# Reordering the opening of a fused Fourier-mixing and gated-cosine kernel on Trainium2: x by two queues first, z's first column group ahead, weight folds inside the steps

## The chip, the cores and the metric

The kernel runs on one core of one Trainium2 chip. The metric is the device time of one execution in microseconds. Before the change three runs gave 1979.25, 1980.98 and 1982.95 us, a median of 1980.98 us.

## The reference

Two parts are computed one after the other, all in float32. x has the shape (8, 3008, 256).

```
X = fft(fft(x, axis=1), axis=2);  y = real(X)            # 8 x 3008 x 256
h = y.reshape(24064, 256) @ w_in                         # w_in 256 x 2048
g = h * cos(h)
out = g @ w_out                                          # w_out 2048 x 256
```

## The kernel before, in words

**How the work is split.** A sequence of 3008 is 47 times 64, so the transform along the sequence is done in two halves. The *first half* multiplies by a table L of 47-point cosines and sines: x is laid out with the 47 index s2 on the partitions (rows 0 to 46 hold 32 of the 64 positions s1, the next 47 rows hold the mirrored other ones), four tiles `xp` of eight positions each per batch, and each tile is two chunks. For a chunk, `fold` (L212) adds and subtracts the mirrored columns of the feature axis into `xf`, `first_half` (L233) makes the products with L into a PSUM bank `pz` and ScalarE copies it to `zs` (L262). z must change its layout, and this goes through DRAM: `store_z` (L268) writes `zs` to `zd`, `load_z` (L280) reads it back as `z2`. The *second half* (`second_half`, L292) multiplies `z2` with the table BJ, one of six column groups g at a time, into `pq`. The transform along the features is folded into the weights: `fold_weights` (L351) multiplies w_in with a cosine and sine table CS into WC and WS, 512 columns (a *quarter*) at a time, and `take_wn` (L364) sums up the row of WS that belongs to the Nyquist feature into `wn` and then lets GpSimd clear that row (L376).

**The steps.** A *step* is one batch b, one column group g and one pair fp of the 16 slices of 128 of the 2048 hidden columns: 8 batches times 6 groups times 8 pairs are 384 steps (L709 to L715). Group 0 has 225 columns, the others 256. In the loop at L724 a step goes through four ages: `seed` (L420, ScalarE writes the Nyquist term and 0.25 into the PSUM bank H), `mm1` (TensorE, L439, cosine part and sine part), `act_e`, `dve_h`, `act_round`, `dve_frac`, `act_sin`, `dve_g`, `dve_s` (ScalarE and VectorE make g times cos for four mirrored outputs), and, three steps later, `mm2` (TensorE, L531: seven products per step, a fast form with the combined weights VX and w2). `combine_w2` (L408) makes VX from w_out on VectorE, a quarter per call.

**What sets the order.** The schedule is manual: the order of the calls is the order on each engine's queue, and every engine works its queue strictly in that order. All loads, and all stores but two at the very end, are issued by SyncE (SP). The work of the next batch's transform is put into the steps by `transform` (L330), and the work of the first batch that isn't needed at once by the table `opening` (L699): its key is a step, and its calls come at the end of that step (L771).

**The opening.** Before the loop stands a list of calls (L642 to L698). SP's order in it is: L, the first x tile, CS, the first quarter of w_in, the second x tile; then the first column group of z (columns 0 to 4 of 24) of chunks 0 and 1; then w_in's second quarter and x tiles 2 and 3; z of chunks 2 and 3; w_in's third quarter, the first part of BJ; then the other columns of z of chunks 0 and 1, and so on; at last the first column group is read back, and after it the rest of z, w_out, the last quarter of w_in and the rest of BJ. TensorE folds the quarters 0, 1 and 2 in this list (L649, L661, L685) and quarter 3 in step 0 (L700, L732). `keep_busy` (L394) gives TensorE products without a use. For group 0 of batch 0 the Nyquist row is spread over the partitions by a product with ones and a ScalarE copy (L320, L323), ahead of the first seed; for all other groups by a store of one row and a load of it to all partitions (L326, L327). The loads of one x tile are, for rows r0 to r1 of 0 to 32 and 32 to 47:

```python
nc.sync.dma_start(
    out=xv[r0:r1], in_=x_r[b, r0:r1, i0 : i0 + XP, :], max_dma_last_dim=2048
)
q0, q1 = N2 + r0, N2 + r1
...
nc.sync.dma_start(
    out=xv[q0:q1], in_=x_r[b, r0:r1, 64 - i0 : 64 - i0 - XP : -1, :]
)
```

so the direct rows lie on partitions 0 to 46 and the mirrored ones on 47 to 93, and the rows of L are in the same order. In the direct part a row of a tile is one run of 8 KB in DRAM, in the mirrored part it is eight runs of 1 KB.

Of the kernel before, what the change touches and what calls it, by code (L numbers as in the profile page):

```python
# [11 lines left out]
FP = mybir.dt.float32  # L12
# [19 lines left out]
def _consts():  # L32
# [19 lines left out]
    L = np.concatenate([LE, LO, LE0, LO0], axis=1)  # L52
    L = np.concatenate([L, np.zeros((128 - 2 * N2, 256))], axis=0)

# [53 lines left out]
def kernel(  # L108
# [30 lines left out]
    def load_x(b, p):  # L139
# [5 lines left out]
        for r0, r1 in ((0, 32), (32, 47)):  # L145
# [3 lines left out]
            q0, q1 = N2 + r0, N2 + r1  # L149
            if p == 0:  # L150
                nc.sync.dma_start(out=xv[q0:q1, 0:1], in_=x_r[b, r0:r1, 32:33, :])
                nc.sync.dma_start(
                    out=xv[q0:q1, 1:XP], in_=x_r[b, r0:r1, 63 : 64 - XP : -1, :]
                )
            else:
                nc.sync.dma_start(
                    out=xv[q0:q1], in_=x_r[b, r0:r1, 64 - i0 : 64 - i0 - XP : -1, :]
                )
# [14 lines left out]
    def load_w(q):  # L173
        for i in range(2):
            nc.sync.dma_start(
# [15 lines left out]

    nc.sync.dma_start(out=L, in_=L_dr.ap())
    load_x(0, 0)
    load_cs()
    load_w(0)
    load_x(0, 1)
# [15 lines left out]
    def fold(b, c, e):  # L212
# [13 lines left out]
        if e:  # L226
            nc.scalar.copy(
# [64 lines left out]
    def second_half(b, g):  # L292
# [25 lines left out]
        if b == 0 and g == 0:  # L318
            pn = psum("pn", "M")
            nc.tensor.matmul(  # L320
                pn[:, 0:T], lhsT=ones, rhs=pq[0:1, T : 2 * T], start=True, stop=True
            )
            nc.scalar.copy(out=nb[:, 0:T], in_=pn[:, 0:T])  # L323
            return
# [3 lines left out]


# [34 lines left out]
    def take_wn(n):  # L364
# [11 lines left out]
        nc.gpsimd.memset(row, 0.0)  # L376

    def fold_quarter(n):
        fold_weights(1, n)
# [40 lines left out]
    def seed(s):  # L420
# [3 lines left out]
        for u in range(2):  # L424
# [7 lines left out]
            )  # L432

# [208 lines left out]
    keep_busy(2, "H", 512)  # L642
    keep_busy(2, "H", 512)
    chunk(0)
    chunk(1)
    first_half(0, 0)
    chunk(2)
    first_half(0, 1)
    fold_weights(1, 0, "H")  # L649
    fold_weights(0, 0, "H")  # L650
    take_wn(0)
    store_z(0, 0, 0, 4)
    store_z(0, 1, 0, 4)
    load_w(1)
    load_x(0, 2)
    load_x(0, 3)
    chunk(3)
    first_half(0, 2)
    chunk(4)
    first_half(0, 3)  # L660
    fold_quarter(1)  # L661
    store_z(0, 2, 0, 4)
    store_z(0, 3, 0, 4)
    x1 = spool.tile([128, XP * ND], FP, tag="xp", bufs=4, name="wr")
    wr.append([x1[:, 1024 * i : 1024 * i + 1024] for i in range(2)])
    load_w(2)
    load_bj(0, 512)
    store_z(0, 0, 4)
    store_z(0, 1, 4)
    chunk(5)  # L670
    first_half(0, 4)
    chunk(6)
    first_half(0, 5)
    store_z(0, 4, 0, 4)
    store_z(0, 5, 0, 4)
    store_z(0, 2, 4)
    store_z(0, 3, 4)
    chunk(7)
    first_half(0, 6)
    first_half(0, 7)  # L680
    store_z(0, 6, 0, 4)
    store_z(0, 7, 0, 4)
    for half in range(2):
        load_z(0, half, 0, 4)
    fold_quarter(2)  # L685
    keep_busy(2, "M", 256)
    load_w2(0, 2)
    load_w(3)
    load_w2(2, 4)
    for c in range(4, 8):  # L690
        store_z(0, c, 4)
    load_bj(512, 1024)
    for half in range(2):
        load_z(0, half, 4)
    load_w2(4, 6)
    load_w2(6, 8)
    load_bj(1024, NJ * 128)
    second_half(0, 0)  # L698
    opening = {  # L699
        0: ((fold_weights, 0, 3), (take_wn, 3), (combine_w2, 0, 2)),  # L700
        1: ((combine_w2, 2, 4),),
        5: ((combine_w2, 4, 6), (second_half, 0, 1)),
        6: ((combine_w2, 6, 8),),
        10: ((second_half, 0, 2), (load_ident,)),
        14: ((second_half, 0, 3),),
        18: ((second_half, 0, 4),),
        22: ((second_half, 0, 5),),
    }
# [96 lines left out]
```

## Time and profile before

| what | value |
|---|---|
| median of 3 runs | 1980.98 us (1979.25 to 1982.95) |
| profiled execution | span 1979.1 us, 28626 instructions; no other time of it is given |
| TensorE (PE) busy | 1951.8 us, 99% of the span |
| VectorE (DVE) busy | 1855.3 us, 94% |
| ScalarE (ACT) busy | 1483.3 us, 75% |
| GpSimd (POOL) busy | 460.8 us, 23% |
| mean granted clock of TensorE | 0.997 of full speed |
| DMA queue of SP | 86.68 MB, 21.3% of 16 engines |
| first product of step 0 (L439) | starts at 44.39 us |
| first product of step 3 (L439) | starts at 58.66 us |
| first product of step 8, the first of group 1 (L439) | starts at 82.43 us |

How to read the profile: a line of the *timeline* has the start, the duration, the engine, the line of the kernel, the operation, the tile written, an arrow and the tiles read, and how many such instructions in a row are put together; brackets give the idle time before it and what ended it. SPq and ACTq are the queues that issue DMAs, and a duration there is that of the issuing alone. *Stretches* give, for a part of the span, its length, then for TensorE's products (PE), TensorE's weight loads (PEld), VectorE, ScalarE and GpSimd the busy time with the number of instructions, then the granted clock of TensorE, the share of the time in which the 16 DMA engines had a transfer (it can pass 1 where transfers overlap on an engine), and GB/s. The *chain* is followed back from the last instruction to whatever released each piece; its rows are the start, the duration and what it was. float32 products run in several passes, so one call of the program shows as more than one row. All times are from the start of the span.

### The profile page before, as it was taken

Reading aid. Unit: us, or ns where it says so; the run is one execution under the profiler, and the core shown is the slowest. Engines: PE = TensorE matmul, PEld = TensorE weight load, DVE = VectorE, ACT = ScalarE, POOL = GpSimd, SP = SyncE. Lnnn points to the kernel's source line nnn. Section 1 sums busy time; section 2 is a strip of 40 time slices with the busy share of each in tenths; the row PEclk is TensorE's granted clock in tenths of the full one; section 3 lists DMA queues with packets and bytes.
Section 4 is the critical chain, followed back from the end, with each engine's and each line's share of the span. In section 5 each row is a group of like instructions: output and inputs, shape, how many; then the busy total and the mean of one; then the engine's idle time right before and its main releaser. Section 6 shows DMA issues by size and latency. Waiting matters only on the chain.

```text
span 1979.1 us, 28626 instructions
## 1 busy us (share of the span) xinstructions
PE 1951.8 (99%) x9350; PEld 1703.2 (86%) x9350; DVE 1855.3 (94%) x3208; ACT 1483.3 (75%) x2696; POOL 460.8 (23%) x420
## 2 busy tenths in 40 slices
PE   7999999999999999999999999999999999999998
PEld 4888899888998889888898888988889888898887
DVE  2999989999899998999999999899999999899998
ACT  2777777777777777777877778777777777778775
POOL 0132212331133211323122232123311223112111
PEclk9999999999999999999999999999999999999999
DMA  7512122131112311122121311223012220200000
GB/s 181 108 43 57 31 49 41 34 62 39 43 31 41 58 35 43 36 45 54 31 43 40 64 30 35 44 55 55 19 40 49 50 51 20 47 21 10 18 16 22
DMA packets 181194, 88.63 MB, mean 45 GB/s; under 512 B 103303, under 2 KB 173622, under 8 KB 180918
## 3 DMA queue, kind: packets, MB, share of 16 engines
q1 hardware_dynamic: 180886, 86.68, 21.3%
q8 instruction: 75, 1.23, 0.3%
q14 instruction: 73, 0.60, 0.1%
q10 hardware_dynamic: 160, 0.13, 0.0%
HBM read 49.50 MB, written 37.27 MB: 44 GB/s over the span
## 4 chain that ended last, share of the span: by engine, by line
PE 90%; DVE 5%; DMA 2%; issue 1%; ACT 1%; SPq 1%; DVEq 0%; ACTq 0%
PE M L531 53%; PE H L439 31%; PE pz L246 3%; PE pb L299 2%; DVE r L484 1%; DMA xp<-in_x_dram 1%; DVE S L502 1%; DVE S L504 1%; DVE S L495 1%; DVE h L455 1%; DVE r L474 0%; DMA out_dram<-ob 0%; SPq L633 0%; DVE ob L623 0%; ACT r L470 0%
## 5 line engine op out<-in xcount | busy, mean ns | idle before, releaser
L480 ACT ACTIVATE r<-r 128x1024 f32<-128x1024 f32 (+1 forms) x384 | 398.6, 1038 | 306.0 <-DVE r L474 305.2
L531 PE MATMUL M<-S,VX 128*128 128x256 f32 (+1 forms) x2304 | 612.3, 375 | 0.0
L531 PEld LDWEIGHTS M<-S,VX 128*128 128x128 f32 x2304 | 437.8, 190 | 49.9
L439 PE MATMUL H<-pq,WS 128*128 128x256 f32 (+1 forms) x1536 | 390.0, 376 | 10.2 <-ACT ew L450 9.8
L439 PE MATMUL H<-pq,WC 128*128 128x256 f32 (+1 forms) x1536 | 394.8, 380 | 1.8 <-ACT H L426 1.8
L531 PE MATMUL M<-r,w 128*128 128x256 f32 (+1 forms) x1536 | 388.5, 375 | 0.0
L426 ACT ACTIVATE H<-nb,wn 128x256 f32<-128x256 f32 (+1 forms) x768 | 363.8, 474 | 17.4 <-DVE r L484 4.8
L455 DVE TENSOR_TENSOR h<-ew,H 128x512 f32<-128x512 f32 (+1 forms) x384 | 257.2, 670 | 95.2 <-PE H L439 87.3
L439 PEld LDWEIGHTS H<-pq,WS 128*128 128x128 f32 x1536 | 289.5, 190 | 52.5 <-ACT ew L450 16.3
L531 PEld LDWEIGHTS M<-r,w 128*128 128x128 f32 x1536 | 301.2, 197 | 27.1
L474 DVE SCALAR_TENSOR_TENSOR r<-r,h 128x512 f32<-128x512 f32 (+1 forms) x384 | 310.1, 807 | 0.0
L439 PEld LDWEIGHTS H<-pq,WC 128*128 128x128 f32 x1536 | 283.6, 190 | 30.3 <-ACT H L426 2.5
L220 POOL TENSOR_TENSOR xf<-xp 94x508 f32<-94x508 f32 x112 | 165.2, 1495 | 565.9 <-PE pz L253 550.1
L495 DVE TENSOR_TENSOR S<-r 128x512 f32<-128x512 f32 (+1 forms) x384 | 290.9, 758 | 0.1
L484 DVE SCALAR_TENSOR_TENSOR r<-h,r 128x512 f32<-128x512 f32 (+1 forms) x384 | 273.8, 713 | 0.0
L470 ACT ACTIVATE r<-H 128x512 f32<-128x512 f32 (+1 forms) x384 | 222.8, 580 | 56.5 <-DVE h L455 53.4
L450 ACT ACTIVATE ew<-H 128x512 f32<-128x512 f32 (+1 forms) x384 | 225.3, 587 | 48.5 <-PE H L439 44.2
L474 DVE SCALAR_TENSOR_TENSOR r<-r,H 128x512 f32<-128x512 f32 (+1 forms) x384 | 255.6, 666 | 0.0
L484 DVE SCALAR_TENSOR_TENSOR r<-H,r 128x512 f32<-128x512 f32 (+1 forms) x384 | 254.5, 663 | 0.3 <-ACT r L480 0.3
L470 ACT ACTIVATE r<-h 128x512 f32<-128x512 f32 (+1 forms) x384 | 236.2, 615 | 0.0
L531 PE MATMUL M<-r,VX 128*128 128x256 f32 (+1 forms) x768 | 225.2, 375 | 0.0
L531 PE MATMUL M<-S,w 128*128 128x256 f32 (+1 forms) x768 | 225.2, 375 | 0.0
(67 smaller groups left out, 1497.6 us busy)
## 6 DMA issues: line engine op xcount, KB each, us to landing
out_dram<-ob SPq DMA_DIRECT2D x728, 32.0 KB
xp<-in_x_dram SPq DMA_DIRECT2D x56, 256.0 KB
zd<-zs SPq DMA_DIRECT2D x112, 96.0 KB
z<-zd SPq DMA_DIRECT2D x28, 384.0 KB
xp<-in_x_dram SPq DMA_DIRECT2D x56, 120.0 KB
nb<-nd SPq DMA_DIRECT2D x40, 128.0 KB
wr<-in_moe_w_in_dram SPq DMA_DIRECT2D x8, 256.0 KB
w<-in_moe_w_out_dram SPq DMA_DIRECT2D x4, 512.0 KB
```

Of the source, the lines that this page charges most:

```text
L220: (nc.gpsimd if b else nc.vector).tensor_tensor(out=fv[:, e, :, 1:128], in0=xv[:, :, 1:128], in1=xv[:, :, 255:128:-1], op=ALU.subtract if ...
L246: nc.tensor.matmul(pz[rows, a:512], lhsT=w, rhs=fv[:, e, a:512], start=True, stop=True)
L426: nc.scalar.activation(out=s.H[:, u * T : u * T + T], in_=s.nb[:, 0:T], func=AF.Copy, bias=0.25, scale=wn[:, f : f + 1],)
L439: nc.tensor.matmul(s.H[:, u * T : u * T + T], lhsT=W[:, 128 * f : 128 * f + 128], rhs=s.pq[:, e * T : e * T + T], start=False, stop=True, ...
L450: nc.scalar.mul(out=s.ew[:, 0 : 2 * s.T], in_=s.H[:, 0 : 2 * s.T], mul=2.0)
L455: nc.vector.tensor_tensor(out=s.h[:, 0 : 2 * T].rearrange("p (u t) -> p u t", u=2)[:, :, ::-1], in0=s.ew[:, 0 : 2 * T].rearrange("p (u t) ...
L470: nc.scalar.activation(out=r, in_=h, func=AF.Copy, bias=BIG, scale=1.0)
L474: nc.vector.scalar_tensor_tensor(out=r, in0=r, scalar=-BIG, in1=h, op0=ALU.add, op1=ALU.subtract)
L480: nc.scalar.activation(out=r, in_=r, func=AF.Sin, bias=0.0, scale=SIN_SCALE)
L484: nc.vector.scalar_tensor_tensor(out=r, in0=h, scalar=-0.25, in1=r, op0=ALU.add, op1=ALU.mult)
L495: nc.vector.tensor_tensor(out=sv[:, 0:2], in0=gv[:, 2:3].to_broadcast([128, 2, T]), in1=gv[:, 0:4:3], op=ALU.subtract,)
L531: nc.tensor.matmul(acc[key][m // 2][:, 256 * (m % 2) : 256 * (m % 2) + T], lhsT=w, rhs=a, start=first, stop=s.fp == 7, skip_group_check=True,)
```

## The change

Seven things change, all but one before or in the first steps.

1. The x loads of batch 0 are the first DMAs of the program, all four tiles, and the mirrored rows are issued by ScalarE's queue instead of SP's (`back`). L comes after the first tile, then CS, the first quarter of w_in and the first part of BJ. For the other batches SP still issues all.
2. The mirrored rows lie elsewhere: those of rows 0 to 31 on partitions 62 to 93, those of rows 32 to 46 on partitions 47 to 61. The rows of the table L are put in the same order. This holds for all batches.
3. For batch 0 the small copy of two columns into `xf` (L227) is GpSimd's and not ScalarE's.
4. The list of calls is a loop over the eight chunks: fold of the next chunk, first half of this one, store of its first column group. After chunk 1 ScalarE's queue issues the second quarter of w_in. After the loop SP reads the first column group back, then come w_out's first part, w_in's quarters 2 and 3, w_out's second part, the rest of z, and the rest of w_out and BJ.
5. Quarter 0 of the weights is folded after the last chunk; quarters 1, 2 and 3 are folded in steps 0, 1 and 2 (`fold_weights(1, t + 1)` in the middle, `fold_rest` at the end of the step).
6. The first step is not seeded by ScalarE: VectorE fills its bank with 0.25 (`fill_first`), and two products of the one Nyquist row of WS with the Nyquist row of `pq` add the term (`seed_first`); the row of WS is cleared after that (`clear_row`). The spreading of the Nyquist row for the later steps of group 0 moves into step 0 (`spread_norm`).
7. `keep_busy` has one product per call instead of two at the start and none later; in `opening` the second half of group 1 moves from step 5 to step 6, and `combine_w2` of the second quarter of w_out stays in step 1.

```diff
--- before.py
+++ after.py
@@ -50,6 +50,7 @@
     LE0 = stack(np.cos(th), z, z, np.cos(thh))
     LO0 = stack(np.sin(th), z, z, np.sin(thh))
     L = np.concatenate([LE, LO, LE0, LO0], axis=1)
+    L = L[np.r_[0:N2, N2 + 32 : 2 * N2, N2 : N2 + 32]]
     L = np.concatenate([L, np.zeros((128 - 2 * N2, 256))], axis=0)
 
     k2 = np.arange(64)
@@ -142,18 +143,18 @@
         xt = xs[b, p]
         xv = xt.rearrange("r (i d) -> r i d", d=ND)
         i0 = XP * p
-        for r0, r1 in ((0, 32), (32, 47)):
+        back = nc.sync if b else nc.scalar
+        for r0, r1, q0, q1 in ((0, 32, 62, 94), (32, 47, 47, 62)):
             nc.sync.dma_start(
                 out=xv[r0:r1], in_=x_r[b, r0:r1, i0 : i0 + XP, :], max_dma_last_dim=2048
             )
-            q0, q1 = N2 + r0, N2 + r1
             if p == 0:
-                nc.sync.dma_start(out=xv[q0:q1, 0:1], in_=x_r[b, r0:r1, 32:33, :])
-                nc.sync.dma_start(
+                back.dma_start(
                     out=xv[q0:q1, 1:XP], in_=x_r[b, r0:r1, 63 : 64 - XP : -1, :]
                 )
+                back.dma_start(out=xv[q0:q1, 0:1], in_=x_r[b, r0:r1, 32:33, :])
             else:
-                nc.sync.dma_start(
+                back.dma_start(
                     out=xv[q0:q1], in_=x_r[b, r0:r1, 64 - i0 : 64 - i0 - XP : -1, :]
                 )
 
@@ -170,9 +171,9 @@
         for i in range(2):
             nc.sync.dma_start(out=CS[i], in_=CS_dr.ap()[i * 128 : (i + 1) * 128, :])
 
-    def load_w(q):
+    def load_w(q, queue=nc.sync):
         for i in range(2):
-            nc.sync.dma_start(
+            queue.dma_start(
                 out=wr[q // 2][i][:, 512 * (q % 2) : 512 * (q % 2) + 512],
                 in_=moe_w_in[i * 128 : (i + 1) * 128, 512 * q : 512 * q + 512],
             )
@@ -189,11 +190,13 @@
             in_=moe_w_out.rearrange("(q p) c -> p q c", p=128)[:, 2 * f0 : 2 * f1],
         )
 
+    load_x(0, 0)
     nc.sync.dma_start(out=L, in_=L_dr.ap())
-    load_x(0, 0)
+    for p in range(1, 4):
+        load_x(0, p)
     load_cs()
     load_w(0)
-    load_x(0, 1)
+    load_bj(0, 512)
     WC = cpool.tile([128, NDFF], FP, tag="WC", name="WC")
     WS = cpool.tile([128, NDFF], FP, tag="WS", name="WS")
     wn = cpool.tile([128, 16], FP, tag="wn", name="wn")
@@ -224,7 +227,7 @@
             op=ALU.subtract if e else ALU.add,
         )
         if e:
-            nc.scalar.copy(
+            (nc.scalar.copy if b else nc.gpsimd.tensor_copy)(
                 out=fv[:, :, :, 0].rearrange("r e i -> r i e"), in_=xv[:, :, 0:129:128]
             )
 
@@ -316,16 +319,18 @@
         nb = spool.tile([128, 256], FP, tag="nb", bufs=8, name="nb")
         ready[b, g] = (pq, nb)
         if b == 0 and g == 0:
-            pn = psum("pn", "M")
-            nc.tensor.matmul(
-                pn[:, 0:T], lhsT=ones, rhs=pq[0:1, T : 2 * T], start=True, stop=True
-            )
-            nc.scalar.copy(out=nb[:, 0:T], in_=pn[:, 0:T])
             return
         nd = dpool.tile([1, 256], FP, tag="nd", bufs=4, name="nd")
         nc.sync.dma_start(out=nd[:, 0:T], in_=pq[0:1, T : 2 * T])
         nc.sync.dma_start(out=nb[:, 0:T], in_=nd[0:1, 0:T].to_broadcast([128, T]))
 
+
+    def spread_norm():
+        T = _width(0)
+        pq, nb = ready[0, 0]
+        pn = psum("pn", "M")
+        nc.tensor.matmul(pn[:, 0:T], lhsT=ones, rhs=pq[0:1, T : 2 * T], start=True, stop=True)
+        nc.scalar.copy(out=nb[:, 0:T], in_=pn[:, 0:T])
 
     def transform(b):
         todo = {}
@@ -373,10 +378,13 @@
                 stop=True,
             )
         nc.scalar.copy(out=wn[:, 4 * n : 4 * n + 4], in_=pw[:, 0:4])
-        nc.gpsimd.memset(row, 0.0)
-
-    def fold_quarter(n):
-        fold_weights(1, n)
+        if n:
+            clear_row(n)
+
+    def clear_row(n):
+        nc.gpsimd.memset(WS[0:1, 512 * n : 512 * n + 512], 0.0)
+
+    def fold_rest(n):
         fold_weights(0, n)
         take_wn(n)
 
@@ -430,6 +438,24 @@
                 bias=0.25,
                 scale=wn[:, f : f + 1],
             )
+
+    def fill_first(s):
+        s.H = psum("H", "H")
+        nc.vector.memset(s.H[:, 0 : 2 * s.T], 0.25)
+
+    def seed_first(s):
+        T = s.T
+        s.pq, s.nb = ready[s.b, s.grp]
+        for u in range(2):
+            nc.tensor.matmul(
+                s.H[:, u * T : u * T + T],
+                lhsT=WS[0:1, 128 * u : 128 * u + 128],
+                rhs=s.pq[0:1, T : 2 * T],
+                start=False,
+                stop=True,
+                skip_group_check=True,
+            )
+        clear_row(0)
 
     def mm1(s, e):
         T = s.T
@@ -639,73 +665,6 @@
         fold(0, c, 0)
         fold(0, c, 1)
 
-    keep_busy(2, "H", 512)
-    keep_busy(2, "H", 512)
-    chunk(0)
-    chunk(1)
-    first_half(0, 0)
-    chunk(2)
-    first_half(0, 1)
-    fold_weights(1, 0, "H")
-    fold_weights(0, 0, "H")
-    take_wn(0)
-    store_z(0, 0, 0, 4)
-    store_z(0, 1, 0, 4)
-    load_w(1)
-    load_x(0, 2)
-    load_x(0, 3)
-    chunk(3)
-    first_half(0, 2)
-    chunk(4)
-    first_half(0, 3)
-    fold_quarter(1)
-    store_z(0, 2, 0, 4)
-    store_z(0, 3, 0, 4)
-    x1 = spool.tile([128, XP * ND], FP, tag="xp", bufs=4, name="wr")
-    wr.append([x1[:, 1024 * i : 1024 * i + 1024] for i in range(2)])
-    load_w(2)
-    load_bj(0, 512)
-    store_z(0, 0, 4)
-    store_z(0, 1, 4)
-    chunk(5)
-    first_half(0, 4)
-    chunk(6)
-    first_half(0, 5)
-    store_z(0, 4, 0, 4)
-    store_z(0, 5, 0, 4)
-    store_z(0, 2, 4)
-    store_z(0, 3, 4)
-    chunk(7)
-    first_half(0, 6)
-    first_half(0, 7)
-    store_z(0, 6, 0, 4)
-    store_z(0, 7, 0, 4)
-    for half in range(2):
-        load_z(0, half, 0, 4)
-    fold_quarter(2)
-    keep_busy(2, "M", 256)
-    load_w2(0, 2)
-    load_w(3)
-    load_w2(2, 4)
-    for c in range(4, 8):
-        store_z(0, c, 4)
-    load_bj(512, 1024)
-    for half in range(2):
-        load_z(0, half, 4)
-    load_w2(4, 6)
-    load_w2(6, 8)
-    load_bj(1024, NJ * 128)
-    second_half(0, 0)
-    opening = {
-        0: ((fold_weights, 0, 3), (take_wn, 3), (combine_w2, 0, 2)),
-        1: ((combine_w2, 2, 4),),
-        5: ((combine_w2, 4, 6), (second_half, 0, 1)),
-        6: ((combine_w2, 6, 8),),
-        10: ((second_half, 0, 2), (load_ident,)),
-        14: ((second_half, 0, 3),),
-        18: ((second_half, 0, 4),),
-        22: ((second_half, 0, 5),),
-    }
     steps = []
     for b in range(NB):
         for g in range(NG):
@@ -713,6 +672,50 @@
                 s = Step()
                 s.b, s.grp, s.fp, s.T = b, g, fp, _width(g)
                 steps.append(s)
+
+    keep_busy(1, "H", 512)
+    keep_busy(1, "H", 512)
+    chunk(0)
+    for c in range(NCH):
+        if c + 1 < NCH:
+            chunk(c + 1)
+        first_half(0, c)
+        store_z(0, c, 0, 4)
+        if c == 1:
+            load_w(1, nc.scalar)
+    for half in range(2):
+        load_z(0, half, 0, 4)
+    x1 = spool.tile([128, XP * ND], FP, tag="xp", bufs=4, name="wr")
+    wr.append([x1[:, 1024 * i : 1024 * i + 1024] for i in range(2)])
+    load_w2(0, 2)
+    load_w(2)
+    load_w(3)
+    load_w2(2, 4)
+    for c in range(NCH):
+        store_z(0, c, 4)
+    for half in range(2):
+        load_z(0, half, 4)
+    load_w2(4, 6)
+    load_bj(512, 1024)
+    load_w2(6, 8)
+    load_bj(1024, NJ * 128)
+    fold_weights(1, 0, "H")
+    fold_weights(0, 0, "H")
+    take_wn(0)
+    fill_first(steps[0])
+    second_half(0, 0)
+    seed_first(steps[0])
+    opening = {
+        0: ((fold_rest, 1), (combine_w2, 0, 2)),
+        1: ((fold_rest, 2), (combine_w2, 2, 4)),
+        2: ((fold_rest, 3),),
+        5: ((combine_w2, 4, 6),),
+        6: ((second_half, 0, 1), (combine_w2, 6, 8)),
+        10: ((second_half, 0, 2), (load_ident,)),
+        14: ((second_half, 0, 3),),
+        18: ((second_half, 0, 4),),
+        22: ((second_half, 0, 5),),
+    }
     per = NG * 8
     n = len(steps)
 
@@ -720,7 +723,6 @@
         s = steps[t] if 0 <= t < n else None
         return s if s is not None and (last is None or s.fp == 7) else None
 
-    seed(steps[0])
     for t in range(n + LAG + 1):
         cur, prev, old, done = step(t), step(t - 1), step(t - 2), step(t - LAG)
         if cur:
@@ -729,7 +731,9 @@
             mm1(cur, 0)
             act_e(cur)
             if t == 0:
-                fold_weights(1, 3)
+                spread_norm()
+            if t < 3:
+                fold_weights(1, t + 1)
         if t - LAG - 1 == n - 1:
             combine_last(steps[n - 1])
             break
```

## The prediction

> **What bounds the kernel now.** I read the page first (busy shares, the 40 slices, the chain of waits), then the chain, the stretches and the queues' order of the first 62 us.
>
> ```profile
> PE   7999999999999999999999999999999999999998
> DVE  2999989999899998999999999899999999899998
> DMA  7512122131112311122121311223012220200000
> GB/s 181 108 43 57 31 49 41 34 62 39 43 31 41 58 35 43 36 45 54 31 43 40 64 30 35 44 55 55 19 40 49 50 51 20 47 21 10 18 16 22
> ```
>
> From the second slice on TensorE is full and the change touches nothing there: PE is 90% of the chain. Only the first slice (49.5 us) is limited otherwise, by transfers. Its chain, from the answer on the first 62 us:
>
> ```profile
> 2.57 4.60 DMA xp<-in_x_dram
> 8.06 6.35 DMA xp<-in_x_dram
> ...
> 16.27 4.49 DMA wr<-in_moe_w_in_dram
> 20.77 8.46 DMA xp<-in_x_dram
> 30.48 4.26 DMA zd<-zs
> 36.33 1.48 DMA zd<-zs
> 38.31 1.95 DMA z<-zd
> ...
> 44.39 1.22 PE H L439 x4
> ```
>
> Loads of x come first, then the way of z out to DRAM and back; step 0's first product starts at 44.39 us. Why x's last tile is used only at 29.35 (VectorE's L220) is seen in the stretches (busy times of the engines, granted clock, DMA share, GB/s) and in SP's queue:
>
> ```profile
> 5.00:7.50 2.50, 2.50 (x4) 1.01 (x3) 0.00 (x0) 0.00 (x0) 0.00 (x0) 1.00 1.12 181
> 7.50:10.00 2.50, 1.95 (x10) 0.96 (x9) 2.08 (x4) 0.32 (x2) 0.00 (x0) 1.00 1.07 328
> 10.00:12.50 2.50, 2.50 (x15) 1.22 (x13) 0.40 (x1) 0.58 (x1) 0.00 (x0) 1.00 1.07 178
> 12.50:15.00 2.50, 2.50 (x7) 0.94 (x5) 0.47 (x1) 0.50 (x2) 0.00 (x0) 1.00 0.31 39
> 15.00:17.50 2.50, 2.00 (x13) 1.30 (x14) 2.00 (x4) 1.42 (x5) 0.51 (x1) 1.00 0.34 52
> ```
> ```profile
> 11.16 4.66 SPq L275 DMA_DIRECT2D zd<-zs  x4
> 15.87 0.83 SPq L175 DMA_DIRECT2D wr<-in_moe_w_in_dram  x2
> ```
>
> Two things: from 12.5 to 17.5 the DMA engines are two thirds idle, because SP, in order, stands at z stores of chunks 0 and 1 with the loads of tiles 2 and 3 behind them; and while x is loaded (32 or 15 rows at a time) a full DMA share moves only about 180 GB/s, while CS and w_in, 128 rows at a time, get 328.
>
> **The change, part by part.** *x first, on two queues.* One tile is 256+120 KB direct and as much mirrored, 0.77 MB; four are 3.08 MB, L 0.13, CS 0.26, w_in's first quarter 0.52, BJ's first part 0.26. Now nothing with a wait on compute stands before them on SP; ACT issues the mirrored ten. Delay: before, L and the first tile (0.90 MB) had gone by about 6.2 us (66, 204, 181 GB/s in the first three stretches) and were used at 7.92, so 1.7 us later; bytes begin at about 1.7 us. The rate with two queues into separate row ranges (0-31 and 62-93, before 0-31 and 47-78) is in no row. Bounds: 181 GB/s (the row of x; nothing gained) and 328 (the row of the 128-row loads; the two ranges as good as one full load). Below 181, if the queues disturb each other: 158 was the slowest stretch with a full share (25.0 to 27.5). I take 255, the middle of the two: the transfers keep the x row's shape, but the two ranges together are spread like the 128-row loads.
>
> At 255, x, L and 0.3 MB of CS (SP gets a little ahead): 1.7 + 3.5/0.255 + 1.7 = 17.1 us, against 29.35. CS and the first half of w_in: 3.74/0.255 + 3.4 = 18.1.
>
> The Trainium skill, SBUF — State Buffer, "Door 1: The DMA port swizzle", says that rows 0-31 reach only half of the SBUF ports and rows from 64 the other half, which agrees with 181 against 328 here. Its section "Can I just issue two DMAs to hit both halves?" speaks against the change: two such transfers at once gained 6%. No run shows this yet; by it the sum is rival B's.
>
> *ACT as an issuer.* ACT also copies zs out of PSUM, in order. Its last mirrored issue waits for older transfers (SP's issues at 5 to 8 us already wait for earlier loads, about eight in flight), until some 10 us; then come the table load (1.28) and two zs copies, then w_in's second quarter. By the same limit that waits for w_in's first half, 18.1, and takes 2 x 0.4. Behind it queue six zs copies, 0.58 each, and for them SP's stores and TensorE's PSUM banks: 18.9 + 3.5 = 22.4. By x alone it is 17.1 + 4.4 (before: 29.35 to the last zs copy's end, 33.77) = 21.5. I take 22.4. Where ACT gave up the small xf copies (0.20 each), POOL takes them: between 0.15 (its 128x62 memset) and 1.43 (its 94x508 subtraction), I take 0.3, nearer the small one; at the upper end 1.1 us more at the last chunk.
>
> *Half the warm-up products.* The eight warm-up passes take 6.71 us, 0.85 each, against 0.46 for the weight folds' passes of equal width (8 in 3.70): TensorE starts at half speed. With half of them, and the gap until 18.9, the last chunks may run slow: their L246 passes cost 1.05 us a chunk at full speed, so 0 to 2.1 us for two, I take 1.5: last zs at 23.9.
>
> *z's first group ahead.* Before, SP's last z store started at 36.33, behind later parts of z, 2.6 us after the last zs copy's end; the second half's products came 4.06 us later, at 40.39. Now the last two stores follow the copy directly: 23.9 + 0.3 + 4.06 = 28.3. The fold of quarter 0 (3.70 + 1.05) lies in this gap; its cover fails by under 1 us if the clock stays low. From there to step 0 it was 4.00 us; the norm's spread (L320, L323) and the ACT seed (0.94) go, a memset and two one-row products (0.4) come: 2.4. Step 0 starts at **30.7**, 13.7 us earlier.
>
> *Folds inside steps.* Each of steps 0 to 2 now holds a quarter: fold 3.4, its row sums 1.0, the step's own products 1.5: 5.9, and 0.4 for the spread in step 0; 18.1, with small waits 18.8. Before, 44.39 to 58.66 was 14.3, one quarter in it. So **+4.5** of the gain goes back; step 3 at 49.5, 9.2 us earlier. Each fold's copy (0.58 on ACT) stands before seeds and sines; ACT has under 5 us of work per step of 6. VectorE's weight combining hides here too.
>
> *After step 3.* Before, TensorE got a low clock again (0.79 from 60 to 65) after the thin steps 1 and 2, and step 3 took 5.97 us instead of 4.2; the new steps 1 and 2 are dense: -1.7 (0 if the low stretch returns in step 0). Group 1's half moves from step 5 to 6: its products began at 73.0 and the norm's second transfer was issued at 76.15, with step 8's seed at 81.12. One step (4.2) later, and some 2 us to land, the seed waits until 82.5 to 84, behind it on ACT a sine and two roundings: +1.0 (0 to 2). Weights and the rest of z now come after group 0's load: w_in's third quarter has about 1 MB ahead of it, so at 256 GB/s it is there some 5 us before its fold; z's rest, 2.6 MB more and BJ, at about 53, step 6 ends at 65. No cost; if late, TensorE stands still in order.
>
> Sum: -13.7 + 4.5 - 1.7 + 1.0 = **-9.9 us**. The profiled span is 1979.1 us (all that is given of that execution); the median of the runs is 1981.0, so 1.9 lie around it: 1979.1 - 9.9 + 1.9 = **1971.1**.
>
> **Rivals.** *B: the two queues give no more than one.* For: the DMA share is over 1 already while x loads. Then 3.21/0.181 + 0.52/0.328 + 3.4 = 22.7 for CS and w_in, x the same; the last zs 1.5 + 22.7 + 4.4 = 28.6, 4.7 later than mine: -5.2, **1975.8**. The idle stretch's end alone carries that. This is also the case in which the change does not do what it says. The skill's 6% would give 192 GB/s, some 1 us better.
>
> *F: full rate, 328.* w_in 3.74/0.328 + 3.4 = 14.8; last zs 14.8 + 0.8 + 3.5 = 19.1, no cold chunks: 4.8 earlier, **1966.3**. For it: the 128-row loads do that; against: two queues keep no order to each other.
>
> *C: slower.* The two queues disturb each other while x loads: many 1 KB pieces of one between 2 KB pieces of the other. The 13.7 us of x would have to become 23.6 to eat all, 3.5/23.6 = 148 GB/s; slower by 0.2% (4 us, about what a measurement of this kernel can tell from no change) is 127 GB/s: **1985**. Against: no stretch with a full share is under 158.
>
> *E: the folded steps cost more.* If each of steps 0 to 2 takes 7.8 us, as step 0 did before (44.39 to 52.21, at clock 0.66), the three are 23.4: 4.6 later, 1975.7; together with B 1980.4, no change.
>
> **How the numbers follow.** Mine 0.45 (1969 to 1974), F 0.15, B 0.18, E 0.06, B with E or another loss of that size 0.07, C 0.09. Faster by over 0.2% (under 1977.0): mine, F, most of B (0.13) and of E (0.05), 0.78. Same: the rest of B and E, 0.06, and B with E 0.06: 0.12. Slower: C and 0.01: 0.10. The range leaves out C, half of B with E, and the ends of F: 1965.5 to 1979.0.
>
> **What would show it.** Right: VectorE's last L220 for batch 0 at about 16 to 18 us; over 230 GB/s between 2.5 and 15; step 0's first L439 at 29 to 32; L439 of step 3 at 48 to 51; afterwards the same chain of TensorE. B shows as 180 GB/s and 22 to 23 us. Wrong would be: a later step 0 in spite of early x (ACT's queue then holds zs), steps 0 to 2 far over 19 us, or an ACT idle of over 2 us before step 8's seed.

## The result and the profile after

The changed kernel takes 1986.14 us (median, 1985.34 to 1987.69) against 1980.18 us for the kernel before beside it (1979.25 to 1983.42): ratio 1.0026, interval 1.0018 to 1.0034. It is slower by 0.26%, just more than the 0.2% that a measurement can tell; 1971.1 us was forecast. The profiled execution's span is 1984.0 us, 4.9 more than before.

The page of the changed kernel, busy tenths and GB/s in 40 slices:

```profile
PE   7999999999999999999999999999999999999998
PEclk8999999999999999999999999999999999999999
DMA  8412122121211311122111211222012220200000
GB/s 189 100 40 56 28 46 49 34 57 37 48 32 38 61 35 42 33 46 52 35 43 39 60 36 34 43 56 56 19 39 46 53 51 19 46 23 10 18 16 22
```

TensorE's row is the same as before, the first slice (now 49.6 us) still holds a 7, and its granted clock there fell from 9 to 8. The first slice moves more bytes than before (189 against 181 GB/s, 8 against 7 tenths). So the transfers did come earlier; what it bought must have been lost on TensorE.

The start of each step's first product (L439 before, L465 after, us) shows where:

| step | before | after | difference |
|---|---|---|---|
| 0 | 44.39 | 36.98 | -7.4 |
| 3 | 58.66 | 59.04 | +0.4 |
| 7 | 78.09 | 76.85 | -1.2 |
| 8 | 82.43 | 85.58 | +3.2 |
| 9 | 89.06 | 93.96 | +4.9 |
| 10 | 93.56 | 98.46 | +4.9 |

From step 10 on the distance stays. The opening gained 7.4 us; steps 0 to 2 gave 7.8 back; steps 3 to 6 gained 1.6; steps 7 and 8 lost 6.1 (76.85 to 93.96 is 17.1 us, 78.09 to 89.06 was 11.0).

The chain of waits of the changed kernel up to step 0 (start, length, what):

```profile
0.74 4.70 DMA xp<-in_x_dram
5.46 5.70 DMA xp<-in_x_dram
11.17 9.70 DMA xp<-in_x_dram
20.89 4.46 DMA BJ<-dft_B
...
28.55 1.50 DMA zd<-zs
30.46 1.97 DMA z<-zd
32.56 1.82 PE pb L302 x8
...
37.05 1.80 PE H L465 x4
```

The tail is the planned one: the last store of z starts at 28.55 and the second half's products 4.0 us later, as forecast (4.06). The head is not: x alone fills the chain up to 20.89. Between the two stand the load of BJ's first part and nine issues of z stores on SP (left out above, 0.3 us each): the last zs copy ends at 27.21, and its last store moves 1.3 us later, where 0.3 was forecast. In the trace each DMA raises one of eight semaphores, taken in turn over both queues, and an issue that takes one again waits until its earlier transfer has landed. So SP's load at 5.46 waits for ScalarE's first one (issued at 0.74), and the z stores wait at 25.4 for BJ. The stretches of the head (busy times of PE, PEld, DVE, ACT, POOL, then granted clock, DMA share, GB/s):

```profile
12.50:15.00 2.50, 0.81 (x6) 0.44 (x4) 1.02 (x2) 0.66 (x2) 1.01 (x2) 1.00 1.10 152
15.00:17.50 2.50, 2.50 (x12) 1.06 (x10) 2.05 (x4) 0.00 (x0) 0.89 (x2) 1.00 1.07 180
...
32.50:35.00 2.50, 1.80 (x8) 1.54 (x8) 0.00 (x0) 0.56 (x2) 0.00 (x0) 0.57 0.91 319
...
40.00:45.00 5.00, 5.00 (x11) 2.61 (x12) 0.73 (x2) 1.74 (x5) 0.00 (x0) 0.69 0.70 206
```

The idle stretch of before (0.31 and 0.34 of the DMA engines from 12.5 to 17.5) is gone, the share is over 1, but the rate stays between 152 and 197 GB/s from 5 to 20 us, where 255 was forecast. x's last tile is first used at 21.69 (VectorE's L223), against 29.35 before and 17.1 forecast. The last two lines belong to the second loss: from 32.8 to 43.1 us TensorE has half its clock, after it stood still from 31.2 to 32.6 waiting for z.

The third loss, around step 8, in the timeline of the changed kernel (start, length, engine, line, what; in brackets the idle time before and who ended it):

```profile
75.96 1.05 PE L302 MATMUL pb<-BJ,z 128*128 128x128 f32 x8
76.83 0.95 ACT L506 ACTIVATE r<-r 128x900 f32<-128x900 f32 x1 [1.21 <-DVE r L500]
78.58 0.58 ACT L318 COPY pq<-pb 128x512 f32<-128x512 f32 x1
80.29 0.36 SPq L325 DMA_DIRECT2D nb<-nd  x1
84.54 0.99 ACT L434 ACTIVATE H<-nb,wn 128x256 f32<-128x256 f32 x2 [4.84 <-DMA nb<-nd]
85.58 2.07 PE L465 MATMUL H<-pq,WC 128*128 128x256 f32 x4 [3.65 <-ACT H L434]
```

The same place before the change:

```profile
72.69 0.95 ACT L480 ACTIVATE r<-r 128x900 f32<-128x900 f32 x1 [1.53 <-DVE r L474]
73.01 1.05 PE L299 MATMUL pb<-BJ,z 128*128 128x128 f32 x8
74.44 0.58 ACT L315 COPY pq<-pb 128x512 f32<-128x512 f32 x1
```

In the changed kernel group 1's products end at 77.0. ACT copies them only at 78.58, because a sine (L506) and two roundings (L496), 76.83 to 78.68, are in front of the copy in its order. Before the change the same three stood in front of it, but they had begun 0.3 us ahead of the products; now the sine waits for VectorE and begins 0.9 us after them. SP sends the Nyquist row out at 79.18 and issues its spreading over 128 rows at 80.29; that lands at 84.5, 4.2 us later. From the product to the seed it is 8.6 us, and a step of this part takes 4.2. Before the change the row also took 4.2 us (issued at 76.15, landed at 80.3 by the trace's semaphores), but the seed of step 8 came only at 81.12, so the wait had 0.8 us to spare and did not show. Now TensorE idles 3.65 us, and has half its clock from 84.0 to 90.9: its first products of step 8 take 2.07 us instead of 1.03.

```profile
86.00:88.00 2.00, 2.00 (x6) 1.60 (x6) 1.57 (x3) 1.61 (x4) 0.00 (x0) 0.50 0.48 74
```

### The profile page after: what moved, and what is told of

Its sections match the earlier page's. It is cut to its first block, busy times and chain, and to the rows that moved or that the text cites. A ratio compares the mean times of both kernels' runs of the same rounds, so it can differ in the third digit from the quotient of the medians.

```text
span 1984.0 us, 28634 instructions
## 1 busy us (share of the span) xinstructions
PE 1954.8 (99%) x9346; PEld 1706.1 (86%) x9346; DVE 1855.8 (94%) x3209; ACT 1482.3 (75%) x2686; POOL 466.0 (23%) x428
## 4 chain that ended last, share of the span: by engine, by line
PE 91%; DVE 5%; DMA 2%; issue 1%; ACT 1%; SPq 0%; DVEq 0%; ACTq 0%
PE M L557 53%; PE H L465 31%; PE pz L249 3%; PE pb L302 2%; DVE r L510 1%; DMA xp<-in_x_dram 1%; DVE S L528 1%; DVE S L521 1%; DVE S L530 1%; PE pw L360 1%; DVE r L500 1%; DVE h L481 1%; ACT r L496 0%; DVE ob L649 0%; SPq L659 0%
## 5 line engine op out<-in xcount | busy, mean ns | idle before, releaser
L506 ACT ACTIVATE r<-r 128x1024 f32<-128x1024 f32 (+1 forms) x384 | 398.4, 1038 | 300.5 <-DVE r L500 299.4
L465 PE MATMUL H<-pq,WC 128*128 128x256 f32 (+1 forms) x1536 | 395.8, 380 | 3.7 <-ACT H L434 3.7
L465 PE MATMUL H<-pq,WS 128*128 128x256 f32 (+1 forms) x1536 | 390.0, 376 | 7.7 <-ACT ew L476 7.4
L465 PEld LDWEIGHTS H<-pq,WS 128*128 128x128 f32 x1536 | 289.9, 190 | 50.5 <-ACT ew L476 14.8
L557 PEld LDWEIGHTS M<-r,w 128*128 128x128 f32 x1536 | 301.2, 197 | 27.2
L465 PEld LDWEIGHTS H<-pq,WC 128*128 128x128 f32 x1536 | 284.0, 191 | 32.4 <-ACT H L434 4.0
L223 POOL TENSOR_TENSOR xf<-xp 94x508 f32<-94x508 f32 x112 | 165.3, 1495 | 563.9 <-PE pz L256 558.0
L496 ACT ACTIVATE r<-H 128x512 f32<-128x512 f32 (+1 forms) x384 | 223.2, 581 | 59.3 <-DVE h L481 56.6
L496 ACT ACTIVATE r<-h 128x512 f32<-128x512 f32 (+1 forms) x384 | 236.2, 615 | 0.0
```

Of the source, the lines that this page charges most:

```text
L223: (nc.gpsimd if b else nc.vector).tensor_tensor(out=fv[:, e, :, 1:128], in0=xv[:, :, 1:128], in1=xv[:, :, 255:128:-1], op=ALU.subtract if ...
L465: nc.tensor.matmul(s.H[:, u * T : u * T + T], lhsT=W[:, 128 * f : 128 * f + 128], rhs=s.pq[:, e * T : e * T + T], start=False, stop=True, ...
L496: nc.scalar.activation(out=r, in_=h, func=AF.Copy, bias=BIG, scale=1.0)
L506: nc.scalar.activation(out=r, in_=r, func=AF.Sin, bias=0.0, scale=SIN_SCALE)
L557: nc.tensor.matmul(acc[key][m // 2][:, 256 * (m % 2) : 256 * (m % 2) + T], lhsT=w, rhs=a, start=first, stop=s.fp == 7, skip_group_check=True,)
```

## The experiments

All times are medians, and each ratio is to the kernel before, run beside on the same chip. That kernel's median was 1980.18 us beside the changed kernel, 1982.16 beside e1 to e4, 1981.16 beside f1 to f4 and 1981.39 beside g1 to g3. A difference of medians between these sets is therefore uncertain by 1 to 2 us; the ratios are the safer guide. "After" is the changed kernel. The changed kernel, e1, e4 and f1 load x in the same way and first use its last tile at 21.69, 22.21, 22.43 and 21.14 us; a difference of 1.3 us in that time says nothing either.

**Group 1's half back in step 5 (e1).** The theory: the round trip of group 1's row is the largest loss. The rival: the cost lies in the colder, longer opening, and the half's place matters little.

```diff
-        5: ((combine_w2, 4, 6),),
-        6: ((second_half, 0, 1), (combine_w2, 6, 8)),
+        5: ((combine_w2, 4, 6), (second_half, 0, 1)),
+        6: ((combine_w2, 6, 8),),
```

> The changed kernel with group 1's second half put back to the end of step 5. Theory N (the row of norms comes too late): in the changed kernel step 7's first product starts at 76.85 us, 1.2 us earlier than before the change, and step 9's at 93.96, 4.9 later; ScalarE stands 4.84 us before step 8's seed. Without that stall the kernel takes 1980 to 1981.5 us, 5 to 6 us less than the changed one, about as much as before the change. Rival P (the second half costs the same wherever it stands, and VectorE's combining in steps 5 and 6 or the low clock would hold step 8 up as well): 1984 or more.

Measured: 1980.82 us, ratio 0.9990 (0.9982 to 0.9999), 5.3 us under the changed kernel by the medians, 0.36% (7 us) by the ratios. Its timeline:

```profile
73.64 1.05 PE L302 MATMUL pb<-BJ,z 128*128 128x128 f32 x8
76.57 0.36 SPq L325 DMA_DIRECT2D nb<-nd  x1
81.54 0.99 ACT L434 ACTIVATE H<-nb,wn 128x256 f32<-128x256 f32 x2 [0.76 <-DVE r L510]
```

The seed of step 8 now waits for VectorE as before the change, no more for the row: that was issued 5 us ahead. The rest of the change, without this move, is worth 0.1%.

**The same move alone, in the kernel before (e2).**

```diff
-        5: ((combine_w2, 4, 6), (second_half, 0, 1)),
-        6: ((combine_w2, 6, 8),),
+        5: ((combine_w2, 4, 6),),
+        6: ((second_half, 0, 1), (combine_w2, 6, 8)),
```

> The kernel before the change with one edit: group 1's second half at the end of step 6 instead of 5. Theory N: step 8's seed waits for the row, and the kernel takes 1985 to 1987 us, 5 to 7 more than before. Rival P: within 1.5 us of before, since step 8's seed would have some slack there.

Measured: 1988.41 us, ratio 1.0028 (1.0017 to 1.0040). The span is 6.0 longer, ACT waits 4.8 us for the row, and step 9 starts at 95.00 instead of 89.06:

```profile
85.11 0.99 ACT L426 ACTIVATE H<-nb,wn 128x256 f32<-128x256 f32 x2 [4.81 <-DMA nb<-nd]
```

The move costs some 5 to 7 us in either kernel: shown from both sides.

**One queue instead of two (e3).** Do the two queues carry x faster, or disturb each other?

```diff
-        back = nc.sync if b else nc.scalar
+        back = nc.sync
```

> The changed kernel with all loads of x on SP's queue. Theory Q (the two queues take turns: in the changed kernel x moved at 152 to 197 GB/s between 5 and 20 us, as on one queue before the change): x's last tile is used within 1.5 us of the 21.7 us of the changed kernel, and the time is within 1.5 us of it. Rival (the second queue does help a little, mostly by the issue time saved): the last tile 3 us or more later and the time 2 to 4 us longer.

Measured: 1983.85 us, ratio 1.0010 (1.0001 to 1.0018). The tiles of x are used at 7.73, 12.30, 16.32 and 23.38 (after: 8.20, 13.98, 16.91, 21.69). The first three come earlier with one queue; the last 1.7 us later, since w_in's second quarter, still on ACT's queue, was issued at 13.32, ahead of x's last pieces at 16.85. All in all it was 2 to 3 us faster and not slower. Its eleven runs spread from 1981.16 to 1988.82 us, with mean clocks from 0.997 down to 0.992, and in the profiled one TensorE has half its clock for 3.4 us around step 0 (38.1 to 41.5) where the changed kernel has it for 10.2, though the order of the work is the same. So the gain may be the clock's and not the queue's, and this run left the question open: f4 repeats it without that overtaking.

**TensorE kept busy while z makes its trip (e4).** The theory: half the clock from 32.8 to 43.1 costs some 4 us.

```diff
     take_wn(0)
+    keep_busy(2, "M", 256)
     fill_first(steps[0])
     second_half(0, 0)
+    keep_busy(2, "M", 256)
     seed_first(steps[0])
```

(with e1's edit)

> As e1, and with two TensorE products without use after the sums of quarter 0 and two after the second half of group 0, to fill the gaps of 1.4 us each around it. Theory W (the half clock from 32.8 to 43.1 us costs step 0 some 3 to 4 us: step 0 took 9.8 us where its passes at full clock make 6.3): the clock stays full there and the kernel is 2.5 to 4.5 us faster than e1. Rival (the clock falls all the same, or the time goes into waiting for the transfers of z): within 1 us of e1.

Measured: 1976.66 us, ratio 0.9973 (0.9963 to 0.9983), 4.2 under e1. The granted clock from 35 to 40 us, e1 first, then e4:

```profile
35.00:40.00 5.00, 4.18 (x11) 2.82 (x10) 0.00 (x0) 1.16 (x3) 0.52 (x1) 0.50 0.90 271
```
```profile
35.00:40.00 5.00, 5.00 (x18) 3.25 (x18) 0.00 (x0) 1.59 (x4) 0.52 (x1) 0.84 0.93 283
```

The clock is higher, but not full throughout as the theory had it: 0.84 here, with half the clock from 33.2 to 36.6. Steps 0 to 2 now take 6.9, 6.1 and 6.1, together 19.2 us, where 18.8 was forecast: the folds were priced right, the clock was not.

**Quarter 1's fold in the two gaps (f1).** If TensorE has to be kept busy there, the fold of step 0 can do it.

```diff
     take_wn(0)
+    fold_weights(1, 1)
     fill_first(steps[0])
     second_half(0, 0)
+    fold_weights(0, 1)
     seed_first(steps[0])
     opening = {
-        0: ((fold_rest, 1), (combine_w2, 0, 2)),
+        0: ((take_wn, 1), (combine_w2, 0, 2)),
...
-            if t < 3:
+            if 0 < t < 3:
                 fold_weights(1, t + 1)
```

(with e1's edit)

> As e1, with quarter 1 folded in the two gaps of TensorE around group 0's second half (its sine part after the sums of quarter 0, its cosine part after the second half's products) in place of e4's products without use; only its sums stay in step 0. Theory F (what is folded inside steps 0 to 2 is paid in full by TensorE, what is folded in a gap only by what it exceeds it): step 1 starts at about 42 us where e4 has 44.7, and the time is 2 to 3 us under e4, 1973.5 to 1975. Rival (ScalarE's copies of the folds delay the second half or the first seeds by as much): within 1 us of e4.

Measured: 1972.81 us, ratio 0.9955 (0.9943 to 0.9968), 3.9 under e4, more than expected. Step 0 starts at 35.71 and takes 3.7 us instead of 6.9, so step 1 starts at 39.37 and not at 42, and from 12.5 to 50 us the clock never drops:

```profile
35.00:40.00 5.00, 4.84 (x25) 3.66 (x25) 1.43 (x4) 3.02 (x7) 0.95 (x2) 1.00 0.84 251
```

In these two profiled executions 3.2 us of the distance lie in step 0, which is the fold. Step 0's start, 2.1 us earlier than in e4, goes with x (last tile 1.3 us earlier) and with the clock (no low stretch here); these two were not separated.

**Two tiles of 16 positions instead of four of 8 (f2).** Are the pieces too small for the two row ranges to be written side by side?

```diff
-XP = 2 * IP
+XP = 4 * IP
...
-    for p in range(1, 4):
-        load_x(0, p)
+    load_x(0, 1)
```

(on e4, with two buffers in place of four, and `fold` and `transform` counting chunks by four)

> As e4, with x in two tiles of 16 positions instead of four of 8, so that batch 0's x is ten transfers of up to 512 KB instead of eighteen of up to 256 KB and hardly an issue waits for an older transfer. Theory T (two queues into separate rows do move more at once, as in the changed kernel's stretch of 2.5 to 5 us with 259 GB/s; afterwards the queues took turns because an issue waited for a transfer of the other queue): over 230 GB/s from 2.5 to 12.5 us, x's last tile used at 15 to 18 us, 3 to 5 us under e4. Rival U (two queues move no more than one; the first stretch is the start alone): 160 to 200 GB/s from 5 us on, the last tile used at 21 us or later, within 1.5 us of e4 or slower, because the first chunk waits for more.

Measured: 1977.79 us, ratio 0.9982 (0.9973 to 0.9990). 291 GB/s in the stretch from 2.5, then 193, 161, 179 and 162. The five rates sum to 986, e4's (251, 181, 174, 197, 129) to 932: pieces of twice the size hardly lift the rate. The last tile is used at 22.01, as in e4 (22.43).

**The same with the mirrored rows at their old places (f3)**, 47 to 78 and 79 to 93, and L in its old order.

```diff
-        for r0, r1, q0, q1 in ((0, 32, 62, 94), (32, 47, 47, 62)):
+        for r0, r1, q0, q1 in ((0, 32, 47, 79), (32, 47, 79, 94)):
```

> As f2, with the mirrored rows on partitions 47 to 93 in the old order. Theory R (the place of the rows decides whether two queues overlap): if f2 moves over 230 GB/s, this moves 30 GB/s less and its last tile comes 2 us later. Rival (the place is of no account): the same within 0.7 us. Under U for f2 both are the same anyway.

Measured: 1978.89 us, ratio 0.9987 (0.9978 to 0.9996), with 238, 165, 140, 147 and 165 GB/s; the last tile is used at 23.88, 1.9 later than f2's. So the new rows do carry more, by some 15% (the five rates' sums, 986 against 855), although the theory's condition, over 230 GB/s in f2, was not met. I had expected no difference after f2.

**One queue, with w_in's second quarter behind the other loads (f4).**

```diff
-        back = nc.sync if b else nc.scalar
+        back = nc.sync
...
     load_bj(0, 512)
+    load_w(1)
...
-        if c == 1:
-            load_w(1, nc.scalar)
```

(on e4)

> As e4, with all loads on SP's queue and w_in's second quarter behind BJ's first part, so that nothing comes between x's tiles (in e3 that quarter came ahead of x's last tile). Theory Q (ScalarE's queue brings nothing in the changed kernel): x's last tile used within 1.5 us of e4's 22.4, the time within 1.5 us of e4. Rival: last tile at 25 us or later, 2 us or more slower.

Measured: 1975.14 us, ratio 0.9967 (0.9954 to 0.9979), 1.5 under e4 by the medians, while the two intervals overlap. x is used at 7.63, 12.18, 16.16 and 20.41 (e4: 8.41, 14.55, 17.51, 22.43). No tile comes later from one queue: the second queue brings nothing here, and the tiles keep their order.

**L first, ahead of x (g1 on f2, g3 on e4).** Does L's load between the first pieces of x break up their overlap?

```diff
+    nc.sync.dma_start(out=L, in_=L_dr.ap())
     load_x(0, 0)
-    nc.sync.dma_start(out=L, in_=L_dr.ap())
```

> As f2, with L issued ahead of x instead of behind its first tile. In f2 both queues moved 291 GB/s together from 2.5 to 5 us, and then SP's load of the second tile stood until 7.8 us, when a mirrored load of ScalarE's queue had landed. With L first that wait falls on an earlier transfer. Theory T (two queues move more while both have work; an issue's wait for a transfer of the other queue makes them take turns): SP's second tile is issued by 6 us, over 220 GB/s from 5 to 10 us (f2: 193 and 161), x's last tile used 2 us or more before f2's 22.0, the time 1 to 3 us under f2. Rival (the turns come from the DMA engines themselves): under 190 GB/s from 5 us on as in f2, the time within 0.7 us of f2.

> As e4 (four tiles of 8 positions, two queues), with L issued ahead of x. Theory T: fewer turns, x's last tile used 1 us or more before e4's 22.4, the time 0.5 to 2 us under e4's 1976.7. Rival: the same within 0.7 us, or slower by what L delays the first tile, 0.5 us.

Measured: g1 1979.16 us, ratio 0.9991 (0.9982 to 1.0000), with 220, 227, 136, 172 and 195 GB/s and the last tile at 23.26, 1.4 us slower than f2. g3 1975.30 us, ratio 0.9971 (0.9961 to 0.9982), the last tile at 21.35, 1.1 before e4's. One of them lost and the other won about the same, neither by more than like loads differ, so L's place settles nothing, and the explanation by it is dropped.

**One queue and quarter 1's fold in the gaps (g2: f1 with f4's edits).**

> f1 and f4 together: quarter 1 folded in the gaps, all loads on SP's queue, w_in's second quarter behind BJ's first part. f4 was 1.5 us under e4, f1 3.9 under e4. If the two are independent 1971 to 1972; if the earlier x only lets TensorE wait for w_in's second quarter, as f1's 1972.8.

Measured: 1972.56 us, ratio 0.9958 (0.9946 to 0.9971), the same as f1. Both beat the kernel before by some 0.4% (0.3 to 0.6 by the intervals). That x comes sooner by one queue no longer shows in the time: step 0 starts at 35.20, in f1 at 35.71.

**Which pieces are slow (h1, h2, h3).** x comes in pieces of 32 rows and of 15 rows. h1 (two queues, on e4) and h2 (one queue, on f4) leave out batch 0's 15-row pieces, so rows 32 to 46 of x are missing from what they compute:

```diff
+        if b == 0:
+            (nc.vector if p % 2 else nc.gpsimd).memset(xt[32:62], 0.0)
         for r0, r1, q0, q1 in ((0, 32, 62, 94), (32, 47, 47, 62)):
+            if b == 0 and r0 == 32:
+                continue
```

h3 (two queues, on e4) leaves out the 32-row pieces in the same way, and has to clear all rows first.

> As e4, but batch 0's pieces of 15 rows (0.98 of 3.08 MB) are left out and their rows are set to zero, so part of batch 0 is not computed; only the loading of x is read. Theory P (the pieces of 15 rows are the slow ones, since few rows are written at a time; the pieces of 32 rows on two queues overlap): over 230 GB/s from 2.5 to 10 us and the last tile used by 14 us. Rival V (all pieces alike at 180 GB/s): 1.7 + (2.10 + 0.13 + 0.3)/0.18 + 1.7 = 17.5 us.

> As f4 (all on SP's queue) with the same pieces of 15 rows left out. If a second queue brings something for pieces of 32 rows, this moves 180 to 200 GB/s and uses its last tile 2 us or more after the kernel with two queues; if a queue on its own already overlaps neighbouring transfers into separate rows, within 1 us of it.

> As e4, but batch 0's pieces of 32 rows are left out (zeros in their place), the pieces of 15 rows stay. Theory P: under 140 GB/s while only they move, so their 0.98 MB take 7 us or more. Rival V: 180 GB/s, 5.4 us.

Measured, one run of each: 1967.54, 1968.58 and 1981.72 us (1982.2 for the kernel before; the three have less to load, and h3 waits for its clearing, so these times stand for no version of the kernel). The stretches of h1, of h2 and of h3 tell the rates:

```profile
7.50:10.00 2.50, 2.50 (x11) 0.90 (x10) 0.95 (x2) 0.00 (x0) 0.00 (x0) 1.00 1.09 243
...
12.50:15.00 2.50, 2.50 (x16) 1.38 (x13) 2.50 (x5) 1.17 (x2) 1.06 (x2) 1.00 1.05 388
```
```profile
7.50:10.00 2.50, 2.50 (x7) 0.79 (x7) 0.74 (x2) 0.00 (x0) 0.94 (x2) 1.00 1.10 234
```
```profile
7.50:10.00 2.50, 0.00 (x0) 0.00 (x0) 1.76 (x1) 1.28 (x1) 2.38 (x5) 1.00 1.02 134
```

All four stretches have a full DMA share. h3's stretch before this one, with 161 GB/s, still has L's 128 rows in it. Pieces of 32 rows move at 234 to 243 GB/s with one queue or two, the 128-row loads behind them at 388, and pieces of 15 rows at 134. x's 2.10 MB in 32-row pieces and 0.98 MB in 15-row pieces take 2.10/0.24 + 0.98/0.134 = 16.1 us at these rates, 192 GB/s on average; the changed kernel showed 152 to 197, some 175 on average, so the last tenth stays unexplained. So x is slow mainly by its 15-row pieces. They are also smaller (120 KB against 256), but f2's pieces of twice the size were hardly faster. The second queue gives little: over the four stretches from 2.5 to 12.5, h1 moves 255 GB/s and h2 242, 5% more. When the last tile could be used is not told by h1 and h2, since VectorE works there without a break from the second tile on.

## Why the prediction was wrong

**x at 255 GB/s.** Wrong; rival B's case came, at some 175 GB/s from 5 to 20 us. B had the last z store at 28.9 (measured 28.55) and step 0 at 35.4 (measured 36.98, the rest being the low clock). That B comes so close is in part luck: the last zs copy ended at 27.2, 1.4 us before B's 28.6, and the wait of SP's z stores, in neither sum, took 1.0 of it back. I took the two row ranges as the thing that limits x and chose the middle between the x row and the 128-row row. The ranges do help (f2 against f3), and 32-row pieces alone come near my figure (240), but a third of x's bytes is in 15-row pieces at 134, which I left in one rate with the others. No row of before told them apart, but the sizes of the pieces were known, and two rates with their own bounds should have been carried. The Trainium skill, SBUF — State Buffer, "Can I just issue two DMAs to hit both halves?", says that two transfers at once, one to each half, gained 6% over a single one. The prediction's 192 GB/s by it is nearer to the measured 175 than 255 was. h1 against h2 (5%) is another comparison, since both of these kernels write both row ranges.

**The idle stretch of the DMA engines, and z ahead.** Right: the stretch is gone, the store-to-product way of z took 4.0 of the forecast 4.06 us, and -7.4 us stood at step 0 even at B's rate.

**The low clock.** Not in the forecast. I counted a cold TensorE for the last chunks and, as rival E, for steps 0 to 2, but not for z's trip: TensorE stands still from 31.2 to 32.6 us, and the second half's products and step 0 run at half clock until 43.1. The way from those products to step 0 was 4.4 us instead of 2.4, and steps 0 to 2 took 22.1 instead of 18.8, nearly E's 23.4. e4 takes most of this away and gains 4.2. A smaller slip in the way to step 0: GpSimd's copy for `xf`, put at 0.3 us, took 0.7.

**Folds inside steps, +4.5.** Right in price at full clock (19.2 us in e4), low by 3.3 with the clock above.

**Steps 3 to 6, -1.7.** Right: -1.6.

**Group 1's half one step later, +1.0 (0 to 2).** This is the step that failed and that decides the sign: steps 7 and 8 lost 6.1 in the changed kernel, and the span 6.0 by the move alone (e2). I saw the place and the wait, and mis-sized three parts. The landing after the issue, put at some 2 us, took 4.2, as it already did in the trace of before. ACT's copy was taken to follow the product as before the change (1.4 us from 73.01 to 74.44); one step later the sine and the two roundings in front of it start late, and it takes 2.6 us. And the idle time that this makes is 3.65 us, after which TensorE has half its clock for most of step 8, a price that a wait alone does not show. With this step undone the change is 0.1% faster (e1), which would still have been "no change" by my bound of 0.2%.

**The balance.** Forecast -9.9; the rate and the clock before step 0 +6.3, the clock in steps 0 to 2 +3.3, steps 3 to 6 +0.1, group 1 +5.1: +4.9, what the spans show. B with E was a rival of its own, 1980.4 us with a chance of 0.07. In its sum that case came, and group 1's further +5.1 makes it 1985.5 of the measured 1986.1. E's mechanism came only in part: one step at a low clock (9.8 us) and two at full clock (6.1 each), not three of 7.8. The chance of slower, 0.10, hung on another mechanism (C) that did not occur; the one that did was inside a term whose range ended at +2, far too soon.

**Not settled.** What makes the landing 4.2 us is settled in part by the trace: in the changed kernel a later row, issued at 148.23 with no other load behind it, lands 3.0 us after the issue, and the like row before the change (issued at 143.32) 3.5 us after it. So most of it is the spreading of one 1 KB row to 128 rows, and some 1 us goes with the four loads of batch 1's x issued right behind (80.75 to 82.14). No run moves these loads. When TensorE's clock falls is not settled either. In the traces of all runs here the low stretches last a multiple of 3.41 us (but for the last one, which the end cuts off). The same order of work around step 0 had 10.2 us of it in the changed kernel, 13.7 in e1 and 3.4 in e3, and the standstill of 1.7 us before 14.81 in the changed kernel had none (1.00 in the stretch from 15.0). Why 15-row pieces are so much slower than 32-row ones is not shown either, and why one queue hands over the tiles a little earlier than two is told by no run.

## What to carry to other kernels

When a producer moves one step later, follow its whole round trip in the order of each queue it passes (here the copy on ACT, two issues on SP, and a landing), and set it against the length of a step; if it is longer, add what the idle time does to TensorE's clock. Work that fills a full engine's steps is paid in full, while the same work in a gap that has to exist anyway costs little and helps to keep the clock up (f1: step 0 is 3.2 us shorter for one fold moved out of it). When a load is made of pieces of different shapes, give each shape its own rate before you ask whether a second queue helps.

## What the runs showed of the hardware that was not expected

With a full DMA share the rate went from 134 GB/s (pieces of 15 rows) over 240 (32 rows) to 388 (128 rows). A second queue added 5% (255 against 242). Spreading one 1 KB row over 128 rows took 3.0 to 3.5 us from issue to landing by itself, and 4.2 with loads of x right behind. An idle time of 3.65 us was followed by half the clock for 6.8 us (84.0 to 90.9), one of 3.58 us in e3 by 3.4 us of it, and one of 1.4 us in the thin opening by 10.2 us (32.8 to 43.1); two products of 256 columns in each of two gaps recovered most of the latter, with a gain of 4.2 us.
